# Half-size inverse turns, four row buffers, a list that counts eight DMA semaphores, and filled TensorE waits in a spectral and S4 network

## The chip, the cores and the metric

The kernel runs on one core of a Trainium2 chip. The metric is the device time of one execution in microseconds (us), the median of several. A core has TensorE (PE; its loads of weights are PEld), VectorE (DVE), ScalarE (ACT), GpSimd (POOL) and SyncE (SP). Each takes its own instructions in order; SP and ACT also issue the transfers (DMA) of this kernel. PSUM has eight banks; the kernel's tiles there are one or two banks.

## The reference

Four layers on x, [2048 positions, 512 channels], all in fp32: a spectral layer (A), an S4 layer (B), and both again with the same weights.

```python
def _A_ref(x, w_r, w_i):
    X = rfft2(x) * (w_r + 1j * w_i)
    return irfft2(X, (S, D))

def _B_ref(u, A_re, A_im, B_re, B_im, C_re, C_im, log_dt, Dskip):
    dt = exp(log_dt)[:, None]
    P = exp((dt * A)[:, :, None] * arange(L))
    K = einsum("dn,dnl,dn->dl", C, P, dt * B).real
    y = irfft(rfft(u, 2 * L) * rfft(K, 2 * L))[:L]     # along the positions
    return y + u * Dskip

x = x + _A_ref(_layernorm(x), ...)
x = x + _B_ref(_layernorm(x), ...)
x = x + _A_ref(_layernorm(x), ...)
x = x + _B_ref(_layernorm(x), ...)
```

## The kernel before

Every transform is a product with a table of cosines and sines, split in two: a transform over 128 of the positions, products with twiddled tables over 16, and back. x stays on chip as [128, 16, 512].

The program has two lists. The first (`plan_k`, `plan_a`) builds the S4 kernel K for all channels and runs the first spectral layer; the second (`plan_rest`) runs the first S4 layer (`layer_b(0, 0)`), the second spectral layer (`forward_a`, `group_a`, `inv_a`) and the second S4 layer (`layer_b(1, 140)`). Here r is 0 for the first and 1 for the second layer of a kind.

An S4 layer treats the channels in two halves, e = 0 and 1, of 256 each:

- `norm_b` normalises x into `xn` (in the tile Ya).
- The first transform runs in *turns*. `turn_x` does 32 channels: two products into PSUM (L787) and one VectorE transpose of 32x32 blocks into `place` (L789). For 128 channels of the first half, `forward_b` takes another way: products (L771), copies by ScalarE to a row buffer (L803), a send to memory (L806, `yd`), and `place_b` brings the rows back in another order (L814). So the first half has four turns and the second has eight.
- `group_b` handles 1/8 of the frequencies for one half, eight *groups* to a half. Its steps: the kernel's spectrum, loaded from memory (L895), or for the second half of the first layer computed from rows loaded at L884; the spectrum of the rows (L836); two VectorE products with the kernel's spectrum (L906); two GpSimd sums (L912); the first inverse product (L922); two ScalarE copies back into `place` (L927), and for some channels a send to memory (L931, `vd`).
- The last inverse transform needs all eight groups of a half. `inv_b` does 64 channels: one VectorE transpose of 128x2048 (L972), four products (L978), one VectorE add to x (L985). `back_b` does the channels that were sent to memory: load (L942), products (L947), add (L952). `OUT` says how many go through memory: none and 128 of 256 in the first layer, all 256 and 128 in the last.
- In the first layer `moments_b` then takes the statistics of the next norm (L1005, L1007); in the last `store_x` sends the result out.

The order of all this is made by a planner when the program is built. Each step is a generator that yields what it needs next: engines, ring buffers, and events. `Clock` keeps a modelled time for every engine, buffer and transfer; `Clock.run` picks, among the steps that could start soonest (within `NEAR` of the first), the one of the lowest rank, and emits its instructions. `after(key, n)` waits in that model for the time of n events, `emitted(key, n)` only until n of them have been emitted. The engines then take the instructions in the emitted order, and wait for each other by semaphores. Costs are in `COST`, transfers in `LAND` and `RATE`:

```python
COST = {..., "SP": (0.05, 0, 0)}
LAND, RATE = 2.0, (320e3, 210e3)
...
now = min(t for t, _ in ready) + NEAR
t, p = min((e for e in ready if e[0] <= now), key=lambda e: e[1][:2])
```

Rings are places in big tiles: `t1` and `t2` (two slots each, for the products of L906), `wo` (output of the inverse transposes), `io` (rows from memory), `G` (tables of the second spectral layer, in the part of Y that `place[0]` uses before).

Of the kernel before, what the change touches and what calls it, by code (L numbers as in the profile page):

```python
# [29 lines left out]
RINGB = {"wo": (2048, 2), "io": (1024, 4)}  # L30
# [8 lines left out]
COST = {"PE": (0.01, 1.69, 0.2), "DVE": (0.07, 1.05, 0.13), "ACT": (0.05, 0.84, 0.15), "POOL": (0.14, 2.12, 0.09), "SP": (0.05, 0, 0)}  # L39
LAND, RATE = 2.0, (320e3, 210e3)  # L40
# [3 lines left out]
OUT = (0, 128), (256, 128)  # L44
TURN_X = 8, 8, 2
NEAR = 0.1

# [144 lines left out]
class Clock:  # L192
# [4 lines left out]
    def __init__(self, net, last=None):  # L197
# [3 lines left out]
        self.pools = []  # L201
        if last:
            self.free, self.seen, self.events, self.land, self.table = last.free, last.seen, last.events, last.land, last.table
# [67 lines left out]

    def take(self, engine, start, us):
# [103 lines left out]

    def run(self, plan):

        pieces = [[rank, i, 0.0, (), piece] for i, (rank, piece) in enumerate(plan)]
        while pieces:  # L380
# [3 lines left out]
            t, p = min((e for e in ready if e[0] <= now), key=lambda e: e[1][:2])  # L384
            self.piece = p[4]
# [12 lines left out]
class Net:  # L398
# [129 lines left out]
    def forward_a(self, r, s2, st):  # L528

        nc = self.nc  # L530
        yield ("DVE a" if r else "ACT a"), self.after((id(st), s2 // 4)), self.emitted(("grouped", 0, 1), 8 * r)
# [248 lines left out]
    def turn_x(self, r, e, i):  # L780

        yield "PE p:a", *(self.after(("normed", r, b), 4) for b in range(4)), self.emitted(("turned", r), 4)
# [9 lines left out]
    def forward_b(self, r, b):  # L792

        kind = "f" if r else "a"
        ring = "iy" if r else "t1"
# [8 lines left out]
        self.mark("turned", r)  # L804
        yield "SP"
# [54 lines left out]
    def tables(self):  # L860

        for q in range(8):
            yield "+SP gi"
# [5 lines left out]
    def group_b(self, r, q, e):  # L869
# [8 lines left out]
        yield (f"SP {ring} yk gk" if new else "SP " + ring, turn, self.emitted(("fold", 1), 16 * r),  # L878
# [28 lines left out]
        self.drop(X, kh)  # L907

# [58 lines left out]
    def inv_b(self, r, e, i):  # L967

        nc = self.nc
        yield "DVE wo", self.after(("grouped", r, e), 8), self.emitted(("rows", r, 1), 8)  # L970
        y = self.w("wo", [128, 32, 64])
        nc.vector.transpose(y.rearrange("p r d -> p d r"), self.place[e][:, :, 64 * i:64 * i + 64].rearrange("p k d -> p d k"))  # L972
        yield "PE p:a"
        q = self.psum("a")
        y = y.rearrange("p (s w) d -> p s w d", w=2)
        for h in range(2):
            for w in range(2):
# [15 lines left out]
    @staticmethod  # L993
    def returns(r, e):

        return OUT[r][e] // 32 + 4 - OUT[r][e] // 64
# [472 lines left out]
```

## Time and profile before

| | |
|---|---|
| time, median of 3 runs | 777.3 us (773.32 to 778.66) |
| the profiled execution's own time | 774.83 us |
| its span | 773.0 us |
| mean granted TensorE clock | 0.904 of full speed |
| busy: TensorE, VectorE, ScalarE, GpSimd | 76%, 72%, 52%, 36% |
| DMA | 121.46 MB, mean 157 GB/s |

The profile is one execution. Its views give the busy time of engines in any stretch, the instructions of one engine in order of time with the idle time ahead of each and what ended it, the groups of instructions by line and shape, the waits by who waited for whom, and the chain of work that ended last. Times in them are us from the span's start. One fp32 product appears as two matmul records. A row such as `x4` merges neighbours of one line; its length runs from the first's start to the last's end. The first list ends near 356, the first S4 layer near 502, the second spectral layer near 654.

### The profile page before, as it was taken

To read this page: it belongs to the slowest core of one execution; us is meant where nothing else is said; L and a number is where in the kernel's file an instruction comes from. 1 tells how busy PE (TensorE), PEld (TensorE's weight loads), DVE (VectorE), ACT (ScalarE), POOL (GpSimd) and SP (SyncE) were. 2 spreads that over 40 slices of the span, in tenths; PEclk is the share of its full clock that TensorE was granted. 3 is DMA by queue.
4 is the path that set the end of the run, shared out by engine and by line. 5 is a ranking of instruction groups with operands and counts; after the bars stand their busy time and mean duration, and the time that the engine had idled before them with its cause. 6 is when DMAs were issued, how large, how long until landed. Compare 5 with 4: busy or idle time off the path is not lost. (4 is left out here: it accounts for less than half of the span.)

```text
span 773.0 us, 18527 instructions
## 1 busy us (share of the span) xinstructions
PE 587.4 (76%) x7588; PEld 343.5 (44%) x7588; DVE 559.9 (72%) x907; ACT 404.3 (52%) x654; POOL 280.0 (36%) x275
## 2 busy tenths in 40 slices
PE   4388887877979889885769763498887899657754
PEld 4277555545746444341424221277675544323221
DVE  5967479747776886798756984895767488696674
ACT  5676888877887888862234221185533155213220
POOL 5382256434362442330155232093534100036630
PEclk9699899988998999999888975799988899999997
DMA  9423312623442954449987482300665000648987
GB/s 335 139 83 127 104 48 82 188 68 102 119 120 84 295 163 135 135 155 308 303 244 235 139 294 77 135 2 18 223 224 199 1 2 2 204 139 277 303 263 206
DMA packets 109781, 121.46 MB, mean 157 GB/s; under 512 B 5916, under 2 KB 90912, under 8 KB 109568
## 3 DMA queue, kind: packets, MB, share of 16 engines
q1 hardware_dynamic: 68336, 93.00, 37.8%
q10 hardware_dynamic: 41360, 27.27, 11.3%
q8 instruction: 60, 0.98, 0.5%
q14 instruction: 25, 0.20, 0.1%
HBM read 80.53 MB, written 39.71 MB: 156 GB/s over the span
## 5 line engine op out<-in xcount | busy, mean ns | idle before, releaser
L912 POOL TENSOR_TENSOR apart<-wk 128x512 f32<-128x512 f32 x64 | 79.8, 1271 | 193.5 <-DVE wk L906 192.4
L1196 POOL TENSOR_TENSOR Y<-wk,Y 128x1024 f32<-128x1024 f32 x32 | 65.3, 2041 | 121.6 <-issue 69.7
L906 DVE TENSOR_TENSOR wk<-ps,wk 128x1024 f32<-128x1024 f32 x64 | 74.8, 1222 | 41.2 <-PE ps L836 15.1
L927 ACT COPY Y<-ps 128x512 f32<-128x512 f32 x64 | 34.4, 589 | 114.1 <-PE ps L922 102.8
L922 PE MATMUL ps<-apart,wk 32*64 32x256 f32 x1024 | 49.1, 442 | 35.7 <-POOL apart L912 31.9
L556 PE MATMUL ps<-cRa,wk 128*128 128x256 f32 x128 | 38.2, 425 | 36.7 <-POOL wk L538 35.4
L738 PE MATMUL ps<-cDaT,apart 128*32 128x256 f32 x256 | 59.8, 385 | 3.1 <-DVE x L753 2.4
L1181 DVE SCALAR_TENSOR_TENSOR wk<-wk,ps 128x1024 f32<-128x1024 f32 x32 | 38.8, 1213 | 23.8 <-ACT wk L1179 23.7
L1149 PE MATMUL ps<-wk,Y 96*128 96x512 bf16 x128 | 43.5, 424 | 12.5 <-DVE Y L1192 9.3
L789 DVE STREAM_TRANSPOSE Y<-ps 128x1024 f32<-128x1024 f32 x24 | 42.8, 1886 | 11.8 <-PE ps L787 11.8
L1165 ACT ACTIVATE Y<-ps 128x1024 f32<-128x1024 f32 x48 | 46.4, 1025 | 6.9 <-PE ps L1149 6.3
L922 PEld LDWEIGHTS ps<-apart,wk 32*64 32x64 f32 x1024 | 18.8, 144 | 69.2 <-POOL apart L912 59.3
L1192 DVE TENSOR_TENSOR Y<-ps,Y 128x1024 f32<-128x1024 f32 x32 | 39.0, 1218 | 11.3 <-ACT ps L1185 11.3
L1209 PEld LDWEIGHTS ps<-Y 128*32 128x32 f32 x2048 | 33.8, 119 | 26.2 <-issue 19.4
L1209 PE MATMUL ps<-Y 128*32 128x64 f32 x2048 | 39.1, 234 | 8.3 <-ACT wk L742 3.6
L538 POOL TENSOR_TENSOR wk<-wk 128x256 f32<-128x256 f32 x32 | 26.9, 840 | 51.1 <-ACT wk L511 27.1
L836 PE MATMUL ps<-Y,wk 64*32 64x256 f32 x1024 | 40.3, 431 | 5.1 <-DMA Y<-yd 1.8
L556 PEld LDWEIGHTS ps<-cRa,wk 128*128 128x128 f32 x128 | 24.5, 213 | 41.1 <-POOL wk L538 38.0
L1184 ACT ACTIVATE wk<-wk,quarter 128x1024 f32<-128x1024 f32 x32 | 36.7, 1146 | 10.2 <-DVE wk L1182 7.7
L738 PEld LDWEIGHTS ps<-cDaT,apart 128*32 128x32 f32 x256 | 26.9, 111 | 32.6 <-issue 6.2
L972 DVE STREAM_TRANSPOSE Ya<-Y 128x2048 f32<-128x2048 f32 x8 | 33.6, 4246 | 8.0 <-ACT Y L927 8.0
L1179 ACT ACTIVATE wk<-ps,magic 128x1024 f32<-128x1024 f32 x32 | 35.2, 1119 | 8.1 <-PE ps L1149 3.9
(203 smaller groups left out, 1504.3 us busy)
## 6 DMA issues: line engine op xcount, KB each, us to landing
wk<-khat SPq DMA_DIRECT2D x24, 512.0 KB, 9.3
yk<-wk ACTq DMA_DIRECT2D x32, 256.0 KB, 2.9
Ya<-vd SPq DMA_DIRECT2D x16, 512.0 KB, 7.5
Y<-in_W_dram SPq DMA_DIRECT2D x12, 515.0 KB, 4.8
x<-in_cPa_dram SPq DMA_DIRECT2D x16, 384.0 KB, 2.9
Y<-in_cGa_dram SPq DMA_DIRECT2D x12, 384.0 KB, 6.4
x<-in_W_dram SPq DMA_DIRECT2D x16, 258.0 KB, 3.6
x<-in_A_x_dram SPq DMA_DIRECT2D x8, 512.0 KB, 8.6
```

The lines of the kernel that those rows point to most:

```text
L556: nc.tensor.matmul(p[:, 0:256], pq[:, 128 * i:128 * i + 128], R2[:, 128 * i:128 * i + 256], start=i == 0, stop=i == 1)
L738: nc.tensor.matmul(p[32 * i:32 * i + 32, o:o + 256], self.folded(r, i)[:, b, s2].rearrange("p g m -> p (g m)"), self.DaT[:, b, :], start=b ...
L789: self.nc.vector.transpose(self.place[e][:, :, 32 * i:32 * i + 32].rearrange("p k d -> p d k"), p.rearrange("p (w s d) -> p d s w", w=2, s ...
L836: self.nc.tensor.matmul(X[j][o:o + 32, 256 * c:256 * c + 256], G[i, j, 2 * h + c, :], y[j][i, h, :], start=True, stop=True)
L906: nc.vector.tensor_tensor(t[c], x, kh[:, :, ::-1, :] if c else kh, op=OP.mult)
L912: nc.gpsimd.tensor_tensor(Z[:, :, c], t[0][:, :, c], t[1][:, :, c], op=op)
L922: nc.tensor.matmul(v[j][64 * a:64 * a + 64, h], gi[o:o + 32, j, 4 + 2 * c:6 + 2 * c, :].rearrange("p a m -> p (a m)"), Z[o:o + 32, j, c, : ...
L1149: self.nc.tensor.matmul(p, f[:, c:c + 128], self.oh[:k, o:o + 512], start=True, stop=True)
L1165: nc.scalar.activation(m[:, :, 1024:] if i == 2 else m[:, i, :1024], p.rearrange("p (i m) -> p i m", i=2) if i == 2 else p, AF.Exp)
L1192: nc.vector.tensor_tensor(E[:, 1, :1024], p, m[:, :1024], op=OP.mult)
L1196: nc.gpsimd.tensor_tensor(E[:, 0, :1024], c, m[:, :1024], op=OP.mult)
L1209: nc.tensor.matmul(pk[32 * j:32 * j + 32, 64 * e:64 * e + 64], E1[:, r, i, :], E2[:, r, i], start=r == 0, stop=r == 1)
```

## The change

It has these parts:

- `inv_b` does 32 channels in place of 64: a transpose of 128x1024, two products, an add of 512. The ring `wo` has four slots of half the size. `returns` counts eight pieces to a half.
- `PACE`: in the second half, turn i of `turn_x` may be emitted once i groups have emitted their products (L906). `LATE`: inverse turn i of the first half in the first layer may be emitted once 8 + i groups have.
- In the first layer `forward_b` takes `t1` for its first two row buffers and `t2` for the other two, and ScalarE issues its sends in the same step as the copies.
- The planner counts 0.4 us for each DMA issue and 370 GB/s; rows of under 1024 bytes go at 0.8 of the rate, and a transfer can't start in the model before the eighth one ahead of it has landed (`LANES`).
- `fill`: ahead of a step that needs TensorE, where the planner expects TensorE to wait more than 1.5 us, it emits fp32 products of 128x128x128, whose results nobody reads, for 0.6 of that wait at 0.22 us each. They go to a PSUM bank that no step holds and that the model says is out of use.
- `forward_a` in the second spectral layer asks the planner for ScalarE, which does its norm, in place of VectorE. `HOLD` is 0 and does nothing.

```diff
-RINGB = {"wo": (2048, 2), "io": (1024, 4)}
+RINGB = {"wo": (1024, 4), "io": (1024, 4)}
-COST = {..., "SP": (0.05, 0, 0)}
-LAND, RATE = 2.0, (320e3, 210e3)
+COST = {..., "SP": (0.4, 0, 0)}
+LAND, RATE = 2.0, (370e3, 210e3)
+SMALL = 0.8
+PACE = 1, 1
+LATE = 1, 1
+HOLD = 0
+FILL = 1.5, 0.6, 0.22
+LANES = 8
...
             if ins.opcode.startswith("DMA"):
-                self.land = max(self.land, start) + out.nbytes() / RATE[both]
+                run = min(self.run_of(a) for a, _ in aps)
+                if len(self.lands) >= LANES:
+                    start = max(start, self.lands[-LANES])
+                self.land = max(self.land, start) + out.nbytes() / (RATE[both] * (SMALL if run < 1024 else 1))
                 done = self.land + LAND
+                self.lands.append(done)
...
+    def fill(self, end):
+        start = self.free.get("PE", 0.0)
+        n = int(FILL[1] * (end - start) / FILL[2]) if end - start > FILL[0] else 0
+        if not n or not hasattr(self.net, "Rb"):
+            return
+        taken = [self.boxes(h[3]) for h in self.held.values() if str(h[3].space) == str(PSUM)]
+        banks = [self.net.ps[:, 512 * i:512 * i + 512] for i in range(8)]
+        free = [(max((t for other, t, *_ in self.seen.get(b.tensor.name, ()) if self.meet(self.boxes(b), other)), default=0.0), i) for i, b in enumerate(banks)
+                if not any(self.meet(self.boxes(b), k) for k in taken)]
+        free = [f for f in free if f[0] <= start]
+        if free:
+            bank = banks[min(free)[1]]
+            for _ in range(n):
+                self.net.nc.tensor.matmul(bank[:, :128], self.net.Rb, self.net.Ra[:, 1], start=True, stop=True)
+            self.note(start)
...
             t, p = min((e for e in ready if e[0] <= now), key=lambda e: e[1][:2])
+            if any(isinstance(need, str) and "PE" in need.split() for need in p[3]):
+                self.fill(t)
...
     def forward_a(self, r, s2, st):
-        yield ("DVE a" if r else "ACT a"), ...
+        yield "ACT a", ...
     def turn_x(self, r, e, i):
-        yield "PE p:a", ..., self.emitted(("turned", r), 4)
+        yield "PE p:a", ..., self.emitted(("turned", r), 4), self.emitted(("mult", r), PACE[r] * i * e)
     def forward_b(self, r, b):
-        ring = "iy" if r else "t1"
+        ring = "iy" if r else f"t{1 + b // 2}"
...
+        if not r:
+            self.nc.scalar.dma_start(self.pieces(self.yd[r], b, 4), y)
+            self.mark("sent", r)
+            return
         yield "SP"
         self.nc.sync.dma_start(self.pieces(self.yd[r], b, 4), y)
     def group_b(self, r, q, e):
...
         self.drop(X, kh)
+        self.mark("mult", r)
     def inv_b(self, r, e, i):
-        yield "DVE wo", self.after(("grouped", r, e), 8), self.emitted(("rows", r, 1), 8)
-        y = self.w("wo", [128, 32, 64])
+        first = OUT[r][e] // 32
+        yield "DVE wo", ..., self.emitted(("mult", r), 8 + LATE[r] * (i - first) if not e else 0)
+        y = self.w("wo", [128, 32, 32])
...
-        if r and i % 2:
+        if r and i % 4 == 3:
...
     def returns(r, e):
-        return OUT[r][e] // 32 + 4 - OUT[r][e] // 64
+        return 8
...
     def layer_b(r, o):
                     if i < OUT[r][e] // 32:
                         yield o + 16 + 16 * e + 2 * i, self.back_b(r, e, i)
-                    if OUT[r][e] // 64 <= i < 4:
-                        yield o + 15 + 16 * e + 2 * i, self.inv_b(r, e, i)
+                    else:
+                        yield o + 13 + 16 * e + i, self.inv_b(r, e, i)
```

More of the change, by code (lines that the diff above doesn't have):

```diff
@@ L36 @@
 NORMS = True, False, True, True
-COST = {"PE": (0.01, 1.69, 0.2), "DVE": (0.07, 1.05, 0.13), "ACT": (0.05, 0.84, 0.15), "POOL": (0.14, 2.12, 0.09), "SP": (0.05, 0, 0)}
-LAND, RATE = 2.0, (320e3, 210e3)
+COST = {"PE": (0.01, 1.69, 0.2), "DVE": (0.07, 1.05, 0.13), "ACT": (0.05, 0.84, 0.15), "POOL": (0.14, 2.12, 0.09), "SP": (0.4, 0, 0)}
+LAND, RATE = 2.0, (370e3, 210e3)
+SMALL = 0.8
 RANK = -4, 0.25, 4, 1.1, 24, 0.5, 25, 0.4
@@ L270, in meet, with run_of @@
         return False
+    @staticmethod
+    def run_of(ap):
+        dims = ap.ap if str(ap.space) == str(DRAM) else ap.ap[1:]
+        n = 1
+        for a, b in dims[::-1]:
+            if a != n and b > 1:
+                break
+            n *= b
+        return n * mybir.dt.size(ap.dtype)
     def take(self, engine, start, us):
@@ L530, in forward_a @@
         nc = self.nc
-        yield ("DVE a" if r else "ACT a"), self.after((id(st), s2 // 4)), self.emitted(("grouped", 0, 1), 8 * r)
+        yield "ACT a", self.after((id(st), s2 // 4)), self.emitted(("grouped", 0, 1), 8 * r)
         xn = self.norm(s2, st)
@@ L780, in turn_x @@
     def turn_x(self, r, e, i):
-        yield "PE p:a", *(self.after(("normed", r, b), 4) for b in range(4)), self.emitted(("turned", r), 4)
+        yield "PE p:a", *(self.after(("normed", r, b), 4) for b in range(4)), self.emitted(("turned", r), 4), self.emitted(("mult", r), PACE[r] * i * e)
         p = self.psum("a")
@@ L862, in tables @@
         for q in range(8):
-            yield "+SP gi"
+            yield "+SP gi", self.emitted(("sent", 0), HOLD * (q > 1))
             self.gi[q] = self.w("gi", [128, 2, 8, 32])
@@ L969, in inv_b @@
         nc = self.nc
-        yield "DVE wo", self.after(("grouped", r, e), 8), self.emitted(("rows", r, 1), 8)
-        y = self.w("wo", [128, 32, 64])
-        nc.vector.transpose(y.rearrange("p r d -> p d r"), self.place[e][:, :, 64 * i:64 * i + 64].rearrange("p k d -> p d k"))
+        first = OUT[r][e] // 32
+        yield "DVE wo", self.after(("grouped", r, e), 8), self.emitted(("rows", r, 1), 8), self.emitted(("mult", r), 8 + LATE[r] * (i - first) if not e else 0)
+        y = self.w("wo", [128, 32, 32])
+        nc.vector.transpose(y.rearrange("p r d -> p d r"), self.place[e][:, :, 32 * i:32 * i + 32].rearrange("p k d -> p d k"))
         yield "PE p:a"
[L974 to L977, printed above, removed]
-                nc.tensor.matmul(q[64 * w:64 * w + 64, 512 * h:512 * h + 512], self.RbT[:, w, :], y[:, 8 * h:8 * h + 8, w, :],
-                                 start=True, stop=True)
+        Q = self.psum("a")
+        q = Q[:, :512]
+        for w in range(2):
+            nc.tensor.matmul(q[64 * w:64 * w + 64], self.RbT[:, w, :], y.rearrange("p (s w) d -> p s w d", w=2)[:, :, w, :], start=True, stop=True)
         self.drop(y)
@@ L1237, in turn_k @@
         last = q == 3
-        yield "SP yk" if last else "SP KT", self.after(("stored", q))
+        yield "SP yk" if last else "SP KT", self.after(("stored", q)), self.emitted(("sent", 0), HOLD * last)
         KT = self.w("yk" if last else "KT", [128, 4, 128])
```

13 lines of the change are left out of this document (7 added, 6 removed).

## The prediction

> **What bounds the kernel now.** I read the share of each engine first: none is full, so the limit changes from stage to stage.
>
> ```profile
> PE 587.4 (76%) x7588; PEld 343.5 (44%) x7588; DVE 559.9 (72%) x907; ACT 404.3 (52%) x654; POOL 280.0 (36%) x275
> ```
>
> Then busy time by stretch, cut where the kernel's own steps begin and end (columns: stretch, its length, PE, PEld, DVE, ACT, POOL busy with counts, granted clock, DMA share, GB/s).
>
> ```profile
> 356.00:382.00 26.00, 17.52 (x90) 9.58 (x88) 19.64 (x13) 4.49 (x8) 0.00 (x0) 0.87 0.97 318
> ...
> 416.00:478.00 62.00, 40.89 (x759) 15.08 (x752) 45.32 (x41) 16.13 (x26) 22.34 (x18) 0.81 0.59 196
> 478.00:502.00 24.00, 10.22 (x36) 4.16 (x37) 22.47 (x50) 2.63 (x8) 1.40 (x2) 0.71 0.40 137
> 502.00:654.00 152.00, 135.48 (x1184) 94.70 (x1183) 110.14 (x268) 73.59 (x205) 54.55 (x77) 0.92 0.25 85
> ```
>
> The first 356 us build the S4 kernel and run the first spectral layer, and 502 to 654 is the second spectral layer: TensorE is nine tenths busy there (135.48 of 152.00), so mostly its clock can move it. The two S4 layers, 356 to 502 and 654 to 773, fill no engine: in 416 to 478 VectorE, the fullest, has 45.32 of 62.00. So waits bind there, and I looked for them in the order of time on single engines (columns: start, length, engine, line, form, count, idle before it and what ended it).
>
> ```profile
> 351.49 2.05 ACT L803 COPY wk<-ps 128x512 f32<-128x512 f32 x4 [0.44 <-ACT wk L856]
> 366.05 1.07 ACT L803 COPY wk<-ps 128x512 f32<-128x512 f32 x2 [12.51 <-DMA yd<-wk]
> ```
> ```profile
> 358.57 0.92 SPq L806 DMA_DIRECT2D yd<-wk  x2
> ...
> 367.25 0.92 SPq L806 DMA_DIRECT2D yd<-wk  x1
> ...
> 375.93 2.29 SPq L814 DMA_DIRECT2D Y<-yd  x4
> ```
> ```profile
> 381.98 2.35 DVE L906 TENSOR_TENSOR wk<-ps,wk 128x1024 f32<-128x1024 f32 x2 [1.83 <-PE ps L836]
> ...
> 410.90 4.62 DVE L906 TENSOR_TENSOR wk<-ps,wk 128x1024 f32<-128x1024 f32 x4 [4.12 <-issue]
> ...
> 462.46 2.36 DVE L906 TENSOR_TENSOR wk<-ps,wk 128x1024 f32<-128x1024 f32 x2 [1.72 <-PE ps L836]
> 470.50 2.35 DVE L906 TENSOR_TENSOR wk<-ps,wk 128x1024 f32<-128x1024 f32 x2 [5.69 <-PE ps L836]
> 477.87 8.23 DVE L972 STREAM_TRANSPOSE Ya<-Y 128x2048 f32<-128x2048 f32 x2 [5.01 <-ACT Y L927]
> ```
>
> Three things are to be seen. ScalarE fills two row buffers at 351.49 and then stands 12.51 us until a send (L806) has left; the sends, on SP, were issued at 358.57 and 367.25. The rows come back (L814) from 375.93, and the first frequency product (L906; two instructions to a group) runs at 381.98; the eighth group's ends at 410.90 + 4.62 = 415.5. The second half's eight groups take until 470.50 + 2.35 = 472.9, so 57.3 us. They share VectorE with transposes of 4.2 us (L972), and the last two groups stand 470.50 - 462.46 = 8.0 us apart, with VectorE idle for 5.69 of them. Behind them comes a tail in which VectorE is busy for 22.47 of 24.00.
>
> ```profile
> SPq L665 <- DVE Ya L972: 17.2, 1, 17.2
> ```
> ```profile
> 452.98 0.38 SPq L884 DMA_DIRECT2D wk<-yk  x1
> ```
>
> Part of that 8.0 is a queue: SP stood 17.2 us at a load (L665) whose buffer the big transposes still read, and the last group's rows (L884), which stand behind it, could be asked for only at 452.98.
>
> The clock is the other part. It is granted at 1.0 or at 0.5, in stretches; I summed the seven cold ones between 60 and 346 us, and looked at what stands just ahead of one.
>
> ```profile
> 133.40:136.80 3.40, 3.40 (x74) 1.84 (x66) 2.88 (x6) 2.49 (x4) 2.64 (x2) 0.50 0.00 0
> ...
> sum 37.40, PE 32.69 PEld 20.75 DVE 24.49 ACT 25.03 POOL 18.52; mean PE 4.67 PEld 2.96 DVE 3.50 ACT 3.58 POOL 2.65
> ```
> ```profile
> 131.91 0.38 PE L1149 MATMUL ps<-wk,Y 96*128 96x512 bf16 x1 [2.03 <-DVE Y L1192]
> ```
> ```profile
> 584.16 1.97 PE ps L641 x16
> ...
> 587.29 1.07 PE ps L641 x16
> ...
> 594.19 1.97 PE ps L641 x16
> ...
> 606.11 1.98 PE ps L641 x16
> ...
> 609.23 4.85 PE ps L738 x64
> ...
> 616.00 3.59 PE ps L738 x64
> ```
>
> A wait of 2.03 us ends at 131.91, and from 133.4 the clock is 0.50. In the 37.40 us of cold stretches TensorE is busy for 32.69; full clock would save half, 16.3. The last fence is from the chain that ended last: the same 16 products cost 1.97 cold and 1.07 warm, three times, and 64 others 4.85 and 3.59. That is 3 x 0.9 + 1.3 = 4.0 us on the chain itself.
>
> **The change, part by part.**
>
> *Four row buffers, and the first layer's sends from ScalarE.* The wait of 12.51 goes. Each send costs ScalarE an issue, some 0.46 us as the two at 358.57 cost SP 0.92, so 1.8 in all; queued behind it are the next copy and then those for the S4 kernel's rows, and a send that must wait for a free semaphore holds both. SP loses four issues ahead of its loads, which may go sooner. Late next is the DMA: its share is 0.97 in this stretch, with the tables, the rows out and back, and the kernel rows of the products. So the first product comes earlier by 0 (DMA full throughout) to 12.5 us (the whole wait). The two later sends can go some 10 us sooner but share a full DMA; I take **-7**, the middle. The Trainium skill, "DMA: Bandwidth & Descriptors", section "Issuing engines are not separate DMA queues", says that a second issuing engine saves only the time of issuing; the DMA share above agrees, and by that rule alone this term would be 1.8 us of issue and the sum 5.2 us later.
>
> ```profile
> L906 DVE TENSOR_TENSOR wk<-ps,wk 128x1024 f32<-128x1024 f32 x64 | 74.8, 1222 | 41.2 <-PE ps L836 15.1 <-ACT Y L927 12.3 <-POOL apart L912 7.7
> L789 DVE STREAM_TRANSPOSE Y<-ps 128x1024 f32<-128x1024 f32 x24 | 42.8, 1886 | 11.8 <-PE ps L787 11.8
> L972 DVE STREAM_TRANSPOSE Ya<-Y 128x2048 f32<-128x2048 f32 x8 | 33.6, 4246 | 8.0 <-ACT Y L927 8.0
> L952 DVE TENSOR_TENSOR x<-x,ps 128x512 f32<-128x512 f32 x16 | 10.7, 682 | 3.0 <-PE ps L947 2.9
> L985 DVE TENSOR_TENSOR x<-x,ps 128x1024 f32<-128x1024 f32 x8 | 9.8, 1225 | 2.0 <-PE ps L978 2.0
> ```
>
> *Second-half turns (L789) one by one between products.* Seven transposes of 1.89 us leave the start and come between the first half's eight groups, each 2 x 1.22 = 2.4 us on VectorE: 8 x 2.4 + 7 x 1.89 = 32 us of VectorE, in a stretch of 33.5 (381.98 to 415.5) that has gaps. Nothing waits at run time for the new order, since the pace is a rule of the list; but TensorE is in order, and a turn's product then stands ahead of a spectrum. If each transpose landed on the chain, 13.2 less the spare 1.5 were added. I take **+2** (-1.5 to +12).
>
> *Inverse turns halved, and paced by the second half's groups.* 12 transposes of 128x1024 take the place of 6 of 128x2048 in the first layer, and 4 of 2 in the last. The trace has no such transpose out of SBUF: half of 4246 is 2.12 us, the one out of PSUM takes 1.89. I take 2.12, for the same source. An add of 512 takes 0.68 (L952) against 1.23 for 1024 (L985), 0.14 dearer for each pair, 1 us in all. With one of each beside every group, the second half has 8 x (2.4 + 2.12 + 0.68) = 41.6 us of VectorE work, under which the next spectrum is to be hidden. The second spectral layer's tables are asked for behind the last inverse turn, so the 17.2 us stand no longer holds the last group's rows. Bounds: 41.6, and 8 x 8.0 = 64 if every group ran like the last two. I take 48 for 57.3, nearer the full engine because the 8.0 had the queue in it: **-9** (-16 to +7). The tail keeps its transposes (8.23 now, 8.5 then); the first half's moments, done so far between products, must slip into the 5.01 us ahead of 477.87, and nearly fit: **+1** (0 to +5).
>
> *The last layer.*
>
> ```profile
> 678.53 12.37 DVE L789 STREAM_TRANSPOSE Y<-ps 128x1024 f32<-128x1024 f32 x7
> ...
> 726.63 2.35 DVE L906 TENSOR_TENSOR wk<-ps,wk 128x1024 f32<-128x1024 f32 x2 [1.61 <-POOL apart L912]
> ...
> 735.47 4.62 DVE L906 TENSOR_TENSOR wk<-ps,wk 128x1024 f32<-128x1024 f32 x4 [1.50 <-PE ps L836]
> ```
> ```profile
> 753.55 3.68 PE L978 MATMUL ps<-Ya,cRbT 128*64 128x512 f32 x8 [5.35 <-DVE Ya L972]
> ...
> 758.38 1.88 PE L978 MATMUL ps<-Ya,cRbT 128*64 128x512 f32 x8
> ```
>
> Seven turns run here in one block of 12.37 us while the products wait; spread out, they take the same time of VectorE, so only the gaps elsewhere in the first half are won. Between 726.63 and 735.47 two products lie 8.8 us apart, while the list orders memory traffic as if an issue cost SP nothing; with 0.4 us for each it may do better. I take **-4** (-10 to +5). At the end the first inverse takes 3.68 at the cold clock and the next 1.88, and the last piece is half as long; but rows that return through memory bind nearly as late: **-2** (-4 to 0).
>
> *Filling.*
>
> ```profile
> 33.09 2.08 PE L556 MATMUL ps<-cRa,wk 128*128 128x256 f32 x4 [13.12 <-POOL wk L538]
> ...
> 38.10 0.38 PE L564 MATMUL ps<-cRa,wk 128*128 128x128 f32 x2
> 38.32 0.39 PE L565 MATMUL ps<-cRa,wk 128*128 128x128 f32 x2
> ```
>
> A fill is an fp32 128x128x128 product; the list counts 0.22 us for it, and the two records of one such product take 0.22 at full clock (38.10 to 38.32). In the time lines I count some 30 TensorE waits of over 1.5 us, from the 13.12 above to the one ahead of 753.55, 95 us together; 0.6 of that is 57 us of fills. They stand ahead of the waiting product and cost nothing while the wait is as long as planned. On the chain above they can give 3 of 4.0; before 346 us I count a quarter of the 16.3, since other engines pace much of that time: **-7** (0 to -20). Where the wait is shorter than planned, or the clock so cold that 0.6 of it becomes 1.2, they delay TensorE; I charge **+4** (0 to +57, all of them). The Trainium skill, "TensorE: Matmul & The Clock Gate", section "Why this matters for your kernels", has the clock fall after gaps of over about 3 us; the 2.03 us ahead of 133.4 speaks against so high a limit. By that rule few waits of the first stage would need a fill, and the sum would be 3 us later.
>
> *The list's other constants* (0.4 us for an issue, 370 GB/s, eight in flight, ScalarE for the norm) only reorder: 0.
>
> **Sum:** -7 + 2 - 9 + 1 - 4 - 2 - 7 + 4 = -22. The profiled execution took 774.8 us (span 773.0), 2.5 below the median of 777.3 and inside 773.32 to 778.66. 774.8 - 22 = 753.
>
> **Rivals.** *Fuller* (0.10): VectorE is packed (-10 at the start, 0 in the first half, -16 in the second, -7 and -3 in the last layer) and the clock gives 14; with +1 and +4 that is -45, 730. For it: 45.32 of 62.00. Against: two in-order engines would have to meet without gaps.
> *Serial groups* (0.12): each turn lands in the chain from product to product and the DMA holds the start: -2, +8 and -2 for the first three terms, the others as above, -4: 771. For it: 8.0 us from group to group with VectorE idle. Against: that had the queue as one cause.
> *Fills in the way* (0.08; slower): the list's waits aren't the chip's, and fills delay products on the chain. Without the +4 the sum is -26; it turns when 26 of the 57 us land on the chain, and at three quarters (43) gives 792. For it: a cold clock doubles them. Against: TensorE idles for 773 - 587 = 186 us, so most have room.
> *No fills* (0.05), so that the change doesn't do what it says: no bank of PSUM is free, or the list's waits are under 1.5 us. The terms -7 and +4 go: 756.
>
> **How the numbers follow.** The forecast has 0.65, with a spread of its own from 740 to 766. The range, 728 to 772, takes in "fuller" and "serial" and leaves out the slower case and the far ends of the bounds. One per cent, 7.8 us, is about what this kernel's times can tell from no change: faster means under 769.5. Forecast, fuller and no fills give 0.80; serial, 0.12, lies within one per cent; fills in the way, 0.08, are slower.
>
> **What would show it.** ScalarE without the 12.5 us wait, and the first L906 at about 375; at 381 the DMA held it. Second-half transposes alternating with products, the first half's eight groups within 36 us. From the end of the eighth group's product to the sixteenth's 48 us; over 55 means serial groups. A mean clock of over 0.93, for the 0.904 of the table above, and the 16 products of L641 at 1.07 throughout. Fills that end before the releaser of the product behind them; where they end after it, the third rival. The forecast is wrong above all if the second half stays over 55 us.

## Result: 777.3 us before, 747.2 us after

| | before | after |
|---|---|---|
| time, median | 777.3 us (773.32 to 778.66) | 747.24 us (743.59 to 748.35) |
| ratio, with its 95 % interval | | 0.961 (0.956 to 0.966) |
| the profiled execution's own time | 774.83 us | 748.11 us |

The change is worth 30 us by the medians; the two profiled executions, which the views below come from, differ by 26.7 us of span. The forecast of 753 was 6 us too high and its range of 728 to 772 holds the time. It was right in sum, less so in its terms. The profile of the changed kernel, first the busy time of the engines and the group of the fills (L413), then by stretch (columns as before), cut where the same steps begin and end.

```profile
PE 624.4 (84%) x8138; PEld 390.1 (52%) x8138; DVE 556.4 (75%) x923; ACT 405.2 (54%) x654; POOL 279.3 (37%) x275
...
L413 PE MATMUL ps<-cRa,cRb 128*128 128x128 f32 x550 | 69.3, 281 | 3.3 <-DMA cRb<-in_cRb_dram 3.3
```
```profile
376.00:413.00 37.00, 30.36 (x603) 14.99 (x603) 31.93 (x24) 11.37 (x20) 17.75 (x15) 1.00 0.84 258
413.00:455.00 42.00, 38.86 (x775) 19.68 (x758) 38.70 (x32) 15.69 (x23) 20.03 (x17) 1.00 0.67 216
...
652.00:681.00 29.00, 26.98 (x490) 13.53 (x474) 29.00 (x23) 6.45 (x12) 17.10 (x14) 0.96 0.82 253
```

In two stretches VectorE is now full or nearly so: busy for 29.00 of 29.00 us in the last layer's first half (652 to 681), and for 38.70 of 42.00 in the first layer's second half (413 to 455). TensorE's 624.4 us hold 69.3 of unused products, so its 84% is not more work done.

VectorE's instructions in the first layer, in order of time; line numbers have moved (products L906 to L951, turns L789 to L830, inverse turns L972 to L1019, their adds L985 to L1030).

```profile
376.24 2.36 DVE L951 TENSOR_TENSOR wk<-ps,wk 128x1024 f32<-128x1024 f32 x2 [4.35 <-PE ps L881]
378.51 1.93 DVE L830 STREAM_TRANSPOSE Y<-ps 128x1024 f32<-128x1024 f32 x1
...
392.57 2.36 DVE L951 TENSOR_TENSOR wk<-ps,wk 128x1024 f32<-128x1024 f32 x2 [1.14 <-DMA wk<-in_cGb_dram]
...
410.15 4.72 DVE L951 TENSOR_TENSOR wk<-ps,wk 128x1024 f32<-128x1024 f32 x4 [0.38 <-DMA wk<-yk]
...
421.65 2.36 DVE L951 TENSOR_TENSOR wk<-ps,wk 128x1024 f32<-128x1024 f32 x2
...
447.42 2.35 DVE L951 TENSOR_TENSOR wk<-ps,wk 128x1024 f32<-128x1024 f32 x2
449.65 0.72 DVE L1030 TENSOR_TENSOR x<-x,ps 128x512 f32<-128x512 f32 x1
450.25 2.21 DVE L1019 STREAM_TRANSPOSE Ya<-Y 128x1024 f32<-128x1024 f32 x1
452.31 2.33 DVE L951 TENSOR_TENSOR wk<-ps,wk 128x1024 f32<-128x1024 f32 x2
...
455.27 5.32 DVE L1050 BATCH_NORM_STATS2 hm<-x 128x6 f32<-128x256 f32 x16
```

Product, add, transpose, product: from 421.65 on, the groups follow one another some 5 us apart (452.31 - 447.42 = 4.9), and VectorE hardly waits. (Of the four instructions at 410.15, the first two are the eighth group's, the others the ninth's.) The groups of instructions say the same: VectorE's idle time ahead of the products of both layers has fallen from 41.2 us to 15.0, and half-size transposes out of SBUF cost 2.15 each.

```profile
L951 DVE TENSOR_TENSOR wk<-ps,wk 128x1024 f32<-128x1024 f32 x64 | 74.5, 1220 | 15.0 <-PE ps L881 5.3
L1019 DVE STREAM_TRANSPOSE Ya<-Y 128x1024 f32<-128x1024 f32 x16 | 34.1, 2154 | 7.3 <-ACT Y L973 7.3
```

To put the gain in places I cut the profiled execution of every kernel at the same events: the first row copy of the first S4 layer, its first product (L906/L951), the end of the eighth and of the sixteenth group's products, the first transforms of the second spectral layer (second position of `forward_a`), the end of the norm ahead of the last layer, and the same marks there. Each figure is one execution, in us; all the kernels below are in it.

```
               list  start first second tail  spectral last:  first second end    mean
               one         half  half         layer 2  start  half  half         clock
before         351.5 30.5  33.5  57.3   30.2  156.1    14.9   36.9  33.9   28.2   0.904
after          352.1 24.2  36.3  42.1   37.0  147.1    13.1   29.0  37.2   28.2   0.961
again          351.3 25.6  37.4  42.1   35.2  147.6    13.8   29.1  37.1   28.9   0.962
no_fill        355.7 25.2  36.5  41.1   36.3  151.0    13.1   29.0  39.4   27.6   0.912
fill_alone     349.6 29.6  34.1  59.1   31.1  148.3    14.5   35.6  34.0   29.2   0.967
no_late        351.5 26.4  37.0  55.7   31.4  148.9    13.4   30.4  37.6   26.9   0.951
no_pace        354.5 23.0  36.1  41.2   37.8  147.0    12.9   35.6  39.4   26.9   0.957
big_turns      350.2 24.4  37.5  42.6   32.8  146.3    12.9   30.1  36.2   27.1   0.969
old_sends      348.8 25.9  40.6  41.2   36.4  148.3    13.4   29.1  37.4   28.7   0.964
hold           353.1 24.1  44.9  41.6   36.7  148.8    13.5   29.1  36.4   26.9   0.950
late_tables    351.0 25.3  39.1  41.4   32.8  148.8    13.4   29.1  37.1   28.5   0.957
old_list       345.3 27.4  38.0  40.8   34.5  147.9    15.1   29.1  33.1   28.6   0.966
old_list_late  347.7 27.0  37.0  40.9   31.9  151.5    14.5   29.1  33.1   28.7   0.961
split_late     349.7 25.1  36.7  41.2   31.8  148.2    13.0   30.4  37.8   27.1   0.959
```

After less before, the span of 746.3 against 773.0: -15.2 in the second half of the first layer, -7.9 in the first half of the last, -9.0 in the spectral layer, -6.3 and +2.8 up to the eighth group, and two losses, +6.8 in the tail and +3.3 in the last layer's second half. "again" is the changed kernel once more: how far it stands from "after" (1.8 us in the tail, 1.4 at the start) shows what one figure is worth. Single figures can scatter more than that: after, again, no_late, no_pace, big_turns, old_sends, hold and late_tables have the same first list, and reach the first row copy between 348.8 and 354.5; and the profiled execution of big_turns (741.93 us) is 8 us under that kernel's median.

### The profile page after: what moved, and what is told of

It is laid out like the page before. It is cut to its first block, busy times and chain, and to the rows that moved or that the text cites. A ratio compares the mean times of both kernels' runs of the same rounds, so it can differ in the third digit from the quotient of the medians.

```text
span 746.3 us, 19649 instructions
## 1 busy us (share of the span) xinstructions
PE 624.4 (84%) x8138; PEld 390.1 (52%) x8138; DVE 556.4 (75%) x923; ACT 405.2 (54%) x654; POOL 279.3 (37%) x275
## 5 line engine op out<-in xcount | busy, mean ns | idle before, releaser
L951 DVE TENSOR_TENSOR wk<-ps,wk 128x1024 f32<-128x1024 f32 x64 | 74.5, 1220 | 15.0 <-PE ps L881 5.3
L413 PEld LDWEIGHTS ps<-cRa,cRb 128*128 128x128 f32 x550 | 64.3, 193 | 18.4 <-issue 13.1
L413 PE MATMUL ps<-cRa,cRb 128*128 128x128 f32 x550 | 69.3, 281 | 3.3 <-DMA cRb<-in_cRb_dram 3.3
L830 DVE STREAM_TRANSPOSE Y<-ps 128x1024 f32<-128x1024 f32 x24 | 44.4, 1930 | 6.3 <-PE ps L828 6.2
L968 PE MATMUL ps<-apart,wk 32*64 32x256 f32 x1024 | 43.1, 398 | 6.6 <-POOL apart L958 5.7
L1194 PE MATMUL ps<-wk,Y 96*128 96x512 bf16 x128 | 40.5, 394 | 9.2 <-ACT Y L1210 4.6
L597 PE MATMUL ps<-cRa,wk 128*128 128x256 f32 x128 | 35.6, 403 | 14.9 <-POOL wk L579 13.6
L779 PEld LDWEIGHTS ps<-cDaT,apart 128*32 128x32 f32 x256 | 26.7, 111 | 34.9 <-DVE x L794 8.1
L881 PE MATMUL ps<-Y,wk 64*32 64x256 f32 x1024 | 36.3, 392 | 9.4 <-ACT Y L973 4.5
L1019 DVE STREAM_TRANSPOSE Ya<-Y 128x1024 f32<-128x1024 f32 x16 | 34.1, 2154 | 7.3 <-ACT Y L973 7.3
```

The costliest lines, as they stand in the source:

```text
L413: self.net.nc.tensor.matmul(bank[:, :128], self.net.Rb, self.net.Ra[:, 1], start=True, stop=True)
L779: nc.tensor.matmul(p[32 * i:32 * i + 32, o:o + 256], self.folded(r, i)[:, b, s2].rearrange("p g m -> p (g m)"), self.DaT[:, b, :], start=b ...
L830: self.nc.vector.transpose(self.place[e][:, :, 32 * i:32 * i + 32].rearrange("p k d -> p d k"), p.rearrange("p (w s d) -> p d s w", w=2, s ...
L881: self.nc.tensor.matmul(X[j][o:o + 32, 256 * c:256 * c + 256], G[i, j, 2 * h + c, :], y[j][i, h, :], start=True, stop=True)
L951: nc.vector.tensor_tensor(t[c], x, kh[:, :, ::-1, :] if c else kh, op=OP.mult)
L968: nc.tensor.matmul(v[j][64 * a:64 * a + 64, h], gi[o:o + 32, j, 4 + 2 * c:6 + 2 * c, :].rearrange("p a m -> p (a m)"), Z[o:o + 32, j, c, : ...
```

## Experiments

Ratios are to the kernel before on the same chip, with their 95 % intervals. To stand beside them, the changed kernel once more, in the last series:

> The changed kernel itself, as a reference on the same chip as the three others: 0.96 of the kernel before, that is 745 where that takes 776. The stretches of its profile give the spread from run to run: the first half of the first S4 layer 36 to 40 us, the others within 1.

It took 749.92 us (748.5 to 750.79), 0.965 (0.961 to 0.969).

### One part undone: fills, the two paces, the list's constants

**no_fill**

```diff
-FILL = 1.5, 0.6, 0.22
+FILL = 1e9, 0.6, 0.22
```

> The changed kernel without its 275 fill products; all else as it is, though the list may place a few steps otherwise. Theory A (the order of the S4 layers did most of the 30 us, the clock 6 in the second spectral layer and nothing in the first list): about 754, the second spectral layer back from 153 to 158 us, the first list unchanged near 352 us to the first row copy. Theory B (the clock did most): 765 or more, the two halves of the S4 layers losing their gains with the clock back at 0.90. Theory C (the fills are in the way as often as they help): 747 or less.

757.41 us, 0.978 (0.972 to 0.983): against 747.24 and 749.92 the fills are worth 8 to 10 us, and by the ratios 10 to 13; the other parts together keep 2.2 %, 17 us. The mean clock falls back to 0.912 from 0.961.

Where they pay, by the table: 3.9 us in the second spectral layer, where 151.0 stands clear of the 146.3 to 148.9 of the kernels that have fills and early tables. The 3.6 in the first list, the 2.2 in the last layer's second half and a cost of 1.0 in the first layer's second half are no larger than what single figures scatter by. In the spectral layer one group of products shows the clock itself; the same 192 products of L641/L682 in the kernel before, the changed one, and the one without fills (columns: count, busy, mean ns, idle before and its releaser):

```profile
L641 PE MATMUL ps<-Y,Ya 128*64 128x128 f32 x192 | 16.7, 328 | 11.8 <-POOL Ya L601 7.0 <-POOL Ya L632 4.8
```
```profile
L682 PE MATMUL ps<-Y,Ya 128*64 128x128 f32 x192 | 13.1, 278 | 10.1 <-POOL Ya L642 6.0 <-POOL Ya L673 4.0
```
```profile
L682 PE MATMUL ps<-Y,Ya 128*64 128x128 f32 x192 | 14.5, 298 | 11.9 <-POOL Ya L673 6.0 <-POOL Ya L642 5.9
```

328 ns, 278, 298: the other parts bring some of it, the fills the rest. The spectral layer as a whole is 5.1 us shorter than before even without fills (151.0 for 156.1); the move of its norm to ScalarE is one part that could do it, and no run undoes that alone.

**no_late**, the inverse turns not paced:

```diff
-LATE = 1, 1
+LATE = 0, 0
```

> The changed kernel with the first half's inverse turns free once eight groups have their products (LATE 0, 0), still in half size. Theory A (the pace by groups is what packed VectorE): the second half of the first S4 layer goes from 42 us back to 55, 760. Rival (half-size turns alone do it, whatever the pace): it stays under 45, 749.

759.74 us, 0.978 (0.969 to 0.987). The second half goes back to 55.7 us of the 57.3 before, although the turns are half-size. VectorE in order of time:

```profile
419.56 6.24 DVE L1019 STREAM_TRANSPOSE Ya<-Y 128x1024 f32<-128x1024 f32 x3 [2.43 <-ACT Y L973]
...
434.55 2.36 DVE L951 TENSOR_TENSOR wk<-ps,wk 128x1024 f32<-128x1024 f32 x2
...
447.94 1.72 DVE L1050 BATCH_NORM_STATS2 hm<-x 128x6 f32<-128x256 f32 x5
...
465.42 2.36 DVE L951 TENSOR_TENSOR wk<-ps,wk 128x1024 f32<-128x1024 f32 x2 [7.37 <-PE ps L881]
```

From 419.56 to 434.55 there are only inverse transposes and adds and no product: the chain of groups stands still. Then the turns have been used up, and at 465.42 VectorE is idle for 7.37 us before a product. This is shown: the pace, not the size, made the second half. Of the 13.6 us about 4 to 6 come back in the tail (31.4 for 37.0 and 35.2). Moments (L1050) stand here between the products (447.94) that have to be done behind them in the changed kernel (455.27), but they are not the main reason: late_tables, below, leaves all 16 of them behind the products and has a tail of 32.8. Here, as there, the send of the last rows finds a quiet DMA. The tables of the spectral layer were asked for by 445.68, long before it, and the fetch follows that send by 2.3 us (SP, ScalarE, SP):

```profile
445.68 0.39 SPq L636 DMA_DIRECT2D Y<-in_W_dram  x1
```
```profile
475.10 0.37 ACTq L977 DMA_DIRECT2D vd<-Y  x1
```
```profile
477.44 1.75 SPq L988 DMA_DIRECT2D Ya<-vd  x4
```

What is left of the 13.6, some 8 to 10 us, is most of the 10 to 12 us by which the totals differ.

**no_pace**, the second half's turns not paced:

```diff
-PACE = 1, 1
+PACE = 0, 0
```

> The changed kernel with the second-half turns free again (PACE 0, 0). Theory A: the last layer's first half goes from 29 us of eight groups back to about 37, so 755; in the first layer the turns run ahead of the first group as before, whose first half gets 3 us shorter and whose start 5 later. Theory C (the list finds the same order by its other constants): 747.

754.09 us (749.86 to 760.51), 0.975 (0.967 to 0.983), 4 to 7 us more than the changed kernel, with intervals that overlap a little. The last layer's first half is 35.6 us, near the 36.9 of before, and the block is back, in VectorE's instructions in order of time:

```profile
656.99 12.34 DVE L830 STREAM_TRANSPOSE Y<-ps 128x1024 f32<-128x1024 f32 x7
```

In the first layer the first half stays as it was (36.1 for 36.3). That half isn't VectorE's: it was busy for 31.93 of 37.00 us there in the changed kernel (376 to 413 above).

**old_list**, the planner's constants as before:

```diff
-COST = {..., "SP": (0.4, 0, 0)}
-LAND, RATE = 2.0, (370e3, 210e3)
-SMALL = 0.8
+COST = {..., "SP": (0.05, 0, 0)}
+LAND, RATE = 2.0, (320e3, 210e3)
+SMALL = 1
-LANES = 8
+LANES = 10 ** 9
```

> The changed kernel with the old constants of the list (SP 0.05, 320 GB/s, no small rows, no limit of transfers in flight). Theory A (the constants only reorder): 747 within 6, either way. Theory C (the constants made the order): 760 or more, the loads of kernel rows and of the second half's rows standing again behind others on SP.

742.47 us, 0.960 (0.953 to 0.966); by its ratio this run alone can't be told from the changed kernel. The stretches say more, the last layer's second half above all. The four kernels with fills whose first list was made with the old constants reach the first row copy at 345.3, 347.7, 349.6 (fill_alone) and 349.7; those with the new ones at 348.8 to 354.5, on average 3.5 us later. The last layer's second half is 33.1 twice with the old ones (33.9 and 34.0 in the kernel before and fill_alone), 36.2 to 39.4 with the new ones. In return the new ones save some 2 us at each layer's start (27.4 and 27.0 for 23.0 to 26.4; 15.1 and 14.5 for 12.9 to 13.8).

### One part undone: size of the turns, senders, put-off loads, late tables

**big_turns**: 64 channels to an inverse turn again, paced.

```diff
-RINGB = {"wo": (1024, 4), ...}
+RINGB = {"wo": (2048, 2), ...}
-        yield "DVE wo", ..., self.emitted(("mult", r), 8 + LATE[r] * (i - first) if not e else 0)
-        y = self.w("wo", [128, 32, 32])
+        yield "DVE wo", ..., self.emitted(("mult", r), 8 + LATE[r] * 2 * (i - first) if not e else 0)
+        y = self.w("wo", [128, 32, 64])
...
```

> The changed kernel with inverse turns of full size (64 channels, 128x2048), paced at one for each two groups. Theory A (the pace packs VectorE, the size matters little): the second half of the first S4 layer within 3 us of 42, the whole within 3 of 747. Rival (the size does it, since a 4.2 us transpose holds the product behind it): 50 us and 755.

749.78 us (741.93 to 751.65), 0.968 (0.959 to 0.976); the second half 42.6 us. Halving them is not seen to bring anything by itself: the pace does it with either size.

**old_sends**: SP issues the first layer's sends, two row buffers.

```diff
-        ring = "iy" if r else f"t{1 + b // 2}"
+        ring = "iy" if r else "t1"
...
-        if not r:
-            self.nc.scalar.dma_start(self.pieces(self.yd[r], b, 4), y)
-            self.mark("sent", r)
-            return
```

> The changed kernel with the first layer's sends on SP again and two row buffers. Theory A: ScalarE waits again for a send, the first product of that layer comes 6 us later, 752. Rival (the DMA is full there, so the sends can't come sooner, and the gain was the turns that left the start): no difference in the start.

752.63 us (751.76 to 754.39), 0.974 (0.967 to 0.981), a loss of 3 to 5 us that just touches the changed kernel's interval. ScalarE's wait for a send is back, on ScalarE's line below, but not its price: the first product, on VectorE's line, runs 25.9 us behind the first row copy, for 24.2 and 25.6 in the changed kernel and 30.5 before.

```profile
360.13 1.07 ACT L844 COPY wk<-ps 128x512 f32<-128x512 f32 x2 [8.44 <-DMA yd<-wk]
```
```profile
374.70 2.35 DVE L947 TENSOR_TENSOR wk<-ps,wk 128x1024 f32<-128x1024 f32 x2 [4.53 <-DMA yk<-wk]
```

SP's lines show why the wait is shorter than the 12.51 of before, and correct what was said of `HOLD`. First the kernel before, where SP issues all eight tables of the groups (`tables`, L866) and only then the first send, at 358.57; then this run, where SP has issued one table (348.98) when the first send leaves.

```profile
350.40 7.60 SPq L866 DMA_DIRECT2D wk<-in_cGb_dram  x8
```
```profile
353.49 0.46 SPq L847 DMA_DIRECT2D yd<-wk  x1
```

The reason is in the planner: a step whose request is a plain string with a "+" in front may go on at its old time. `HOLD`, even at 0, puts a second need beside that string in `tables`, so the request is a tuple, the "+" has no effect, and each table waits in the model until the one before it has landed. The block of eight is there in the kernel before and in fill_alone (350.24, 6.16 us, x8) and in no kernel with the rest of the change. No run has this edit alone.

Where the loss of 3 to 5 us falls isn't shown. The first half has 40.6 us, but late_tables, with the sends as in the changed kernel, has 39.1; and the eighth group's products end at 415.3 here, for 412.6, 414.3 and 415.4 in after, again and late_tables.

**hold**: loads of S4 kernel rows and their tables put off until the four sends have been emitted.

```diff
-HOLD = 0
+HOLD = 4
```

> The changed kernel with HOLD at 4: the tables and kernel rows of the later groups, and the last rows of the S4 kernel, are asked for only once the four sends are emitted. Theory (the DMA holds the start of the first S4 layer): the first product comes 3 to 6 us sooner. Rival: the start stays at 24 us from the first copy, and what was put off is late for the groups, so the first half gets longer.

755.74 us, 0.978 (0.971 to 0.984). The idea that these loads hold the first product fell: it comes 24.1 us behind the first copy, as in the changed kernel (24.2). The delay lands on the later groups, on VectorE in order of time:

```profile
402.18 2.36 DVE L951 TENSOR_TENSOR wk<-ps,wk 128x1024 f32<-128x1024 f32 x2 [4.43 <-PE ps L881]
```

These are the fourth group's products. They come at 402.18, after 4.43 us of waiting for a spectrum, where they came at 392.57 in the changed kernel; the first half grows to 44.9 us.

**late_tables**: tables of the second spectral layer asked for only when the last inverse turn and return have been emitted.

```diff
     def group_a(self, g):
-        yield "SP G", self.emitted(("inv", 0, int(g > 3)), self.returns(0, int(g > 3)))
+        yield "SP G", self.emitted(("inv", 0, 1), self.returns(0, 1))
     def first_a(self, r, g):
-        yield "SP G", self.emitted(("inv", 0, 0), self.returns(0, 0)) if r else ...
+        yield "SP G", self.emitted(("inv", 0, 1), self.returns(0, 1)) if r else ...
```

> The changed kernel with one difference on SP: the four loads of the second spectral layer's tables (3.6 MB) stand behind the loads of the first layer's returning rows, not ahead of them. Theory (the tail behind the last product grew because the sends and loads of the returning rows now share the DMA with these tables: DMA share 0.99 at 455 to 462, and 7.2 us from the last send to the load behind it for 2.3 before): the tail gets 4 to 6 us shorter, 742. Rival (VectorE's moments, which moved there, made it longer): no difference.

This run was made for the tail. In the changed kernel SP issues eight loads of tables (L706 to L636) just when ScalarE sends the last rows out (L977); the rows can be fetched (L988) only when that send has landed. SP, ScalarE and the stretch by itself, changed kernel:

```profile
452.53 0.33 SPq L706 DMA_DIRECT2D Y<-in_cPa_dram  x1
...
456.05 0.63 SPq L636 DMA_DIRECT2D Y<-in_W_dram  x1
466.44 1.75 SPq L988 DMA_DIRECT2D Ya<-vd  x4
```
```profile
459.20 0.37 ACTq L977 DMA_DIRECT2D vd<-Y  x1
```
```profile
455.00:462.00 7.00, 6.47 (x79) 5.51 (x79) 6.97 (x18) 1.07 (x2) 2.31 (x2) 1.00 0.99 340
```

From 459.20 to 466.44 are 7.2 us, with the DMA at 0.99. Before, a send of the same kind at 477.87 was followed by the fetch at 480.22, 2.3 us later, with the DMA at 0.00 ahead of it:

```profile
477.87 0.37 ACTq L931 DMA_DIRECT2D vd<-Y  x1
```
```profile
480.22 1.94 SPq L942 DMA_DIRECT2D Ya<-vd  x4
```
```profile
473.00:478.00 5.00, 2.32 (x32) 0.67 (x32) 0.13 (x1) 1.07 (x2) 2.48 (x2) 0.50 0.00 0
```

With the tables late it is 2.4 us again, from 461.46 to 463.88, at a DMA share of 0.15:

```profile
461.46 0.37 ACTq L977 DMA_DIRECT2D vd<-Y  x1
```
```profile
463.88 1.75 SPq L988 DMA_DIRECT2D Ya<-vd  x4
```
```profile
455.00:462.00 7.00, 6.46 (x83) 4.30 (x71) 6.97 (x17) 2.15 (x4) 2.50 (x2) 1.00 0.15 40
```

The tail is 32.8 us, and 31.9 and 31.8 in the two kernels below with the same edit, for 37.0 and 35.2. In big_turns, where the tables were asked for 3.5 us earlier (449.06 for 452.53) ahead of a send at the same time, the fetch follows the send by 4.7 us (459.23 to 463.89) and the tail is 32.8. That mechanism is shown. The total doesn't follow: 746.26 us, 0.964 (0.958 to 0.971). In the profiled execution the first half of the first layer took 39.1 and the spectral layer 148.8, for 36.3 and 147.1. Both are within what single figures scatter by, and whether the later tables cost the spectral layer something isn't shown.

### Together, and the fills alone

**old_list_late** is late_tables with the constants of old_list. **split_late** has the old constants for the first list only, with the tables late too:

```diff
+OLD = {"COST": {**COST, "SP": (0.05, 0, 0)}, "RATE": (320e3, 210e3), "SMALL": 1, "LANES": 10 ** 9}
+NEW = {k: globals()[k] for k in OLD}
...
+        globals().update(OLD)     # ahead of the first list
...
+        globals().update(NEW)     # ahead of the second
```

> Both findings together: the old constants of the list (first list 345 us to the first row copy for 352, second half of the last layer 33 for 37) and the second spectral layer's tables behind the returning rows (tail 33 for 37). Theory (stretches add up): 738, 8 under the changed kernel. Rival (what one stretch wins the next gives back, or the profiles differ by chance): within 3 of the changed kernel.

> The old constants for the first list alone, the new ones for the second, and the tables behind the returning rows. Theory (the new constants cost 6 us in the first list and win 3 at the start of the first S4 layer): 736 to 740. Rival (they win nothing after the first list, since the last layer's second half lost 4 with them): 742.

738.94 us (737.33 to 743.26), 0.952 (0.947 to 0.956), and 738.62 (732.36 to 744.87), 0.947 (0.942 to 0.953). Both beat the kernel before by 37 us (776.22 in that series) and, beside it on the same chip, the changed kernel (0.965) by 11, with intervals that don't touch. Which of the two edits brings how much isn't settled: each alone was within the changed kernel's interval. Nor did the new constants earn their place in the second list: the two differ by less than their intervals.

**fill_alone** is the kernel before with `fill` and its call, and nothing else of the change:

```diff
+FILL = 1.5, 0.6, 0.22
...
+    def fill(self, end):
...
+            if any(isinstance(need, str) and "PE" in need.split() for need in p[3]):
+                self.fill(t)
```

> The kernel before, with the fill products added and nothing else of the change. Theory A (fills give some 8 us by the clock, wherever TensorE waits for more than 1.5 us): 768, clock 0.95 or more, the second spectral layer 4 to 8 us shorter and the cold stretch ahead of it gone. Rival (fills pay only with the new order, and get in the way of the old one): 776 or more.

764.61 us (760.35 to 767.03), 0.983 (0.979 to 0.988): 12 us by the fills alone. The profiled execution was the slowest of the six; its span is 7.9 us shorter than before, and the second spectral layer 7.8. And a test of the third rival, the longest fill of the program: TensorE in the changed kernel, then TensorE and GpSimd (whose sum the waiting products need) in this one.

```profile
24.81 8.75 PE L413 MATMUL ps<-cRa,cRb 128*128 128x128 f32 x76 [3.33 <-DMA cRb<-in_cRb_dram]
34.55 1.13 PE L597 MATMUL ps<-cRa,wk 128*128 128x256 f32 x4 [0.99 <-POOL wk L579]
```
```profile
23.77 11.27 PE L392 MATMUL ps<-cRa,cRb 128*128 128x128 f32 x84 [3.03 <-DMA cRb<-in_cRb_dram]
34.88 1.03 PE L576 MATMUL ps<-cRa,wk 128*128 128x256 f32 x4
```
```profile
33.87 0.73 POOL L558 TENSOR_TENSOR wk<-wk 128x256 f32<-128x256 f32 x1 [14.61 <-ACT wk L531]
```

In the changed kernel 76 records fill 8.75 us of the 13, and the product behind them still waits 0.99 us for GpSimd: covered. In fill_alone, at a mean granted clock of 0.85 over the fill, for 1.00 in the changed kernel, 84 records take 11.27 us, to 35.04, where GpSimd was done at 33.87 + 0.73 = 34.60: 0.3 to 0.4 us too long, and no more.

## Why the prediction was right

**Four buffers and sends from ScalarE (-7): size near, cause wrong.** The four copies run without a wait for a send, as forecast:

```profile
352.08 1.05 ACT L844 COPY wk<-ps 128x512 f32<-128x512 f32 x2
...
357.72 1.07 ACT L844 COPY wk<-ps 128x512 f32<-128x512 f32 x2 [0.74 <-PE ps L812]
```

The first product came at 376.24 for 381.98, where "about 375" was to show the forecast and 381 a full DMA; behind the first row copy it came 6.3 us sooner (24.2 for 30.5). But old_sends, without this part, has 25.9, so four buffers and the sender account for 0.3 to 1.7 us of it. The failed step is the one that took the wait of 12.51 for what the first product waited for, and for a matter of buffers and senders. It isn't the fills (25.2 without them) nor the pace (23.0); the list's constants bring some 2 us (27.4 and 27.0 with the old ones). What else changed is that SP no longer issues eight tables ahead of the first send (350.40 before), an effect of `HOLD` that the prediction didn't see; how much that brings isn't measured. By the rule of the Trainium skill that I set beside this term ("DMA: Bandwidth & Descriptors", "Issuing engines are not separate DMA queues") only issue time would be saved, 1.8 us; as far as the first product goes, the 0.3 to 1.7 us of old_sends agree with it.

**First half (+2): size near, mechanism not shown.** 36.3 us for the 36 said, +2.8 over before, with the transposes between the products (378.51 and on). Six moved there and not seven: before, eleven of the twelve stood ahead of the first product and one behind it (384.26), now five and seven. But no_pace, with eight ahead and four behind, has 36.1 too, and VectorE is idle for 5 of the 37 us. That these transposes are what lengthened the half is not shown.

**Second half (-9): right mechanism, too small.** 42.1 us: close to the engine-full bound of 41.6, not the 48 chosen halfway. I had kept distance from it because two in-order engines would have to meet without gaps. Here they nearly do (38.70 of 42.00 busy). The pace is what did it (no_late); the halving, which the term also named, is not (big_turns). I read it from the rows above as a matter of slack: each transpose may slip by a group, so the product always finds its spectrum ready, and there is no idle time in brackets from 447.42 to 452.31. The last group's rows were not held by a load any more, as said: they were asked for at 431.1 (L929), for 452.98 before.

**Tail (+1): mis-sized, +6.8.** The moments, which the term was about, are the smaller part: with the tables late they still stand behind the products, and the tail is 31.8 to 32.8, 1.6 to 2.6 over before. The other 4 to 5 us are a collision that I hadn't seen: I noted that the tables would be asked for behind the last inverse turn, took it as the end of a wait on SP, and did not ask what those loads would meet on the DMA.

**Last layer's groups (-4): right sign, -6.4 with its start.** Spreading seven turns won 7.9 us in the first half (6.6 of them go again in no_pace), where the step "they take the same time of VectorE, so only the gaps elsewhere in the first half are won" had left little. VectorE has none left:

```profile
651.84 4.62 DVE L951 TENSOR_TENSOR wk<-ps,wk 128x1024 f32<-128x1024 f32 x4
656.37 3.79 DVE L830 STREAM_TRANSPOSE Y<-ps 128x1024 f32<-128x1024 f32 x2
660.01 4.59 DVE L951 TENSOR_TENSOR wk<-ps,wk 128x1024 f32<-128x1024 f32 x4
...
697.68 0.69 DVE L998 TENSOR_TENSOR x<-x,ps 128x512 f32<-128x512 f32 x1 [1.76 <-PE ps L993]
```

At 697.68 VectorE waits for products of rows from memory (L993), and the second half is 3.3 us longer than before. The list's constants do that: with the old ones it is 33.1; by which wait isn't shown. So "it may do better", for a planner that counts an issue, was the wrong way round, and "the list's other constants: 0" was wrong by 3 to 4 us in the first list and 4 here, less some 4 at the two starts.

**End (-2): nothing.** 28.2 us, as before. The chain that ended last shows why: it runs through the send of the last rows and their return, and the inverse products wait behind it whatever their clock or size. Before, it ran through the large transpose (749.34, 4.17 us) and the cold products, so that path did get shorter, and the rows from memory, which I had named, bind just as late.

```profile
722.61 2.29 DMA vd<-Y
...
725.02 4.29 DMA Ya<-vd
...
729.44 1.97 PE ps L993 x4
```

**Fills (-7 and +4): both too timid.** Together -3 in the sum, measured -8 to -13 (no_fill, fill_alone). The spectral layer alone gives 4 to 8, where I had read 3 off the chain. I had counted only the four pieces there that can be compared with a warm twin; which others gained I didn't trace. The charge of 4 for fills in the way isn't seen: the one place in the table where they may cost, 42.1 for 41.1 in the second half, is within the scatter, and the longest fill overran by at most 0.4 us. For each of the other fills I can't say. The clock came to 0.961, over the 0.93 said. L641's products (now L682) fell to a mean of 278 ns, from 328, and none of the 192 records is longer than 324: the 16 products ran warm throughout, as said. The Trainium skill ("TensorE: Matmul & The Clock Gate", "Why this matters for your kernels") lets gaps of under about 3 us pass; the planner fills from 1.5 us, and these runs don't tell which of its fills, over or under 3 us, brought the gain. The trace of the kernel before does show the clock fall without a wait of 3 us. At 403.0 it goes from 1.00 to 0.50, with TensorE busy for 1.71 of the 3.39 us just ahead, and its longest wait in the 6.8 us ahead is 1.22 (400.75):

```profile
399.60:402.99 3.39, 1.71 (x48) 0.81 (x56) 2.35 (x2) 0.35 (x2) 3.00 (x3) 1.00 0.76 236
403.03:406.40 3.37, 1.95 (x43) 0.78 (x32) 1.98 (x2) 0.75 (x2) 1.79 (x2) 0.50 0.97 291
```

*Serial groups* needed a second half of over 55 us. no_late has 55.7, but by another way: a block of inverse transposes ahead of the groups (419.56 to 434.55), and not one turn in each chain from product to product. *Fuller* was right in the second half and wrong in the tail and the end.

## What to carry to other kernels

When work off the critical path shares an in-order engine with a chain of small steps, spread it one piece per step: here a rule of one line gave the second half, and the size of the pieces nothing. Behind every wait that goes, look at which transfers it had kept away from a small send on the chain; eight loads cost that send 5 us. Filling planned waits of TensorE with unused products is cheap as long as the plan leaves room, and a planner's constants are worth an experiment of their own. Here 0.4 us for an issue is what the traces show (0.37 to 0.42 at L931 and L977), and yet the set of constants with it had a first list some 3.5 us longer and a last second half some 4 us longer in the profiled executions, though the totals of old_list and the changed kernel can't be told apart. And look at what a switch that is off does to the order of the list: `HOLD` at 0 spread eight loads that had gone out in one block.

## What the runs showed of the hardware

- A store whose rows could be fetched 2.3 to 2.4 us after its issue on a quiet DMA took 7.2 with eight table loads issued within the 7 us ahead of it (459.20 to 466.44, DMA share 0.99).
- VectorE's transposes of 128x1024 take 2.15 us out of SBUF and 1.93 out of PSUM (L1019's group; L830 at 378.51), against 4.25 for the large one before: no price for halving.
- Unused products in TensorE's planned waits raised the mean granted clock from 0.904 to 0.967, with no other edit, and took 1.7 % (1.2 to 2.1) off the time (fill_alone).
